# Odd 64 queries of each batch: one 128-query window per pair replaced by paired 64-column tiles

## The chip, the cores and the metric

The kernel runs on one core of one Trainium2 chip. The metric is the device time of one execution in microseconds. Before the change it is 575.62 us, the median of three runs (575.4 to 577.56 us).

## The reference

A query-and-key-normalised attention over 8 batches, 12 heads, 448 tokens and 64 dimensions per head is followed by a low-rank mixer over the tokens and a two-layer MLP with a ReLU.

```python
q_n, k_n = rmsnorm(q, g_q), rmsnorm(k, g_k)
attn = softmax(q_n @ k_n.T / sqrt(64))
x = (attn @ v)                      # (8, 12, 448, 64), then rows of 768 per token
u = x + (x.T @ U @ V).T             # U (448, 32), V (32, 448): mixes tokens
out = u + relu(u @ w_ch1) @ w_ch2   # 768 -> 3072 -> 768
```

## The kernel before

**Tiling.** Heads are taken in pairs (six a batch) and pairs in groups of two. 448 tokens are three blocks of 128 and one of 64. The exponentials of a pair are one tile `E` with the keys on the partitions and the 448 queries in the columns: two slots for each of three key blocks (one per head), and a seventh slot that holds the last 64 keys of both heads on its two halves. Two `E` buffers take turns.

**Attention products.** `products` (L475) multiplies `E` by the values. The stationary operand is a window of 128 query columns of `E`, the moving one the values with a column of ones (65 columns a head, so that the row sums come with it). A window takes seven matmuls: one of 130 columns for the slot with the last keys (L485) and six of 65 columns (L489). Since 448 is not a multiple of 128, there are four windows per pair, and the fourth overlaps its neighbour by 64 queries: `WIN` (L54) starts it at 320 in even batches and at 0 in odd ones. Half of that window's rows are used. One call of `V` (L504) does two windows and then, on DVE, a reciprocal of the sums (L498) and a multiplication into the batch's rows `x` (L499).

**Scores.** From group 6 on (batch 2), `Spair` (L444) does a pair's scores as one stretch of PE: two 64-row matmuls side by side (L450, tiles `sl`), four more in two rounds (L459, tiles `sc`), and one over all 128 rows (L461, a third `sl`). ACT follows with the exponentials: one for each of the first two `sl` (L452), then the last `sl` (L462), then two double tiles (L464). In batch 1 `Srows` does the same in smaller steps (L429, L434), and batch 0 is written out by hand.

**Mixer and MLP.** `mix_t` (L513) multiplies the batch's rows by `U`, in four 32-column tiles side by side (L518); `mix_two` (L525) multiplies by `V` and adds the rows (L541). `up` (L596) makes one block of the hidden layer: six matmuls of 448 columns (L600) into a tile `ph`, then a ReLU on ACT (L607). `down` (L640) makes a tile `po` of 128 tokens by 384 columns from 24 matmuls (L647), given out in four parts of six, and then adds the rows on DVE (L657).

**PSUM.** Two pools: `ps_sc` with two double buffers (for `sc`), and `ps` with four single buffers, which `ph`, `po`, `pv`, `sl` and the mixer's `pu` share. A tile takes a buffer that has been read out, or the one that will be first.

**Order.** All engines are in the order in which the program records instructions. Two lists are merged: `att` (attention steps, each with a cost) and `mlp` (MLP steps of the batch before). A step of `att` is taken when its share is due (`due`) and `ready` (L898) agrees; otherwise the next MLP step is. `ready` looks at running estimates of each engine's time and keeps scores and `V` apart by at least one MLP step. `done_at` holds the place in `att` from which a batch's rows are complete, and no MLP step of the batch is taken before it.

Of the kernel before, what the change touches and what calls it, by code (L numbers as in the profile page):

```python
# [9 lines left out]
FP32 = mybir.dt.float32  # L10
# [10 lines left out]
LEAD = 1.8  # L21
REST = 8.0
SECOND = 53.0


@with_exitstack
def kernel(
# [413 lines left out]
        runs("act", 0.9 if n == 2 else 0.52)  # L441
        exp_done[(b, pr)] = at["act"]

    def Spair(b, pr):  # L444
        qT, kT = qk[divmod(b * NPAIR + pr, 2)]
        E = es[(b, pr)] = ep.tile([P, NB, S], BF16, name="E", tag="E")
        ts = [ps.tile([P, 512], FP32, name="sl", tag="ps")[:, :S] for _ in range(2)]
        for i in range(2):
            d = slice(i * D, (i + 1) * D)
            nc.tensor.matmul(ts[i], kT[d, 2 * P:3 * P], qT[d], start=True, stop=True)  # L450
        for i in range(2):
            nc.scalar.activation(E[:, 4 + i, :], ts[i], AF.Exp, scale=scal, bias=bias)  # L452
        runs("pe", 0.4)
        runs("act", 1.04)
        tiles = [ps_sc.tile([P, 2, 512], FP32, name="sc", tag="sc") for _ in range(2)]
        for r in range(2):
            for i in range(2):
                d = slice(i * D, (i + 1) * D)
                nc.tensor.matmul(tiles[r][:, i, :S], kT[d, r * P:(r + 1) * P], qT[d], start=True, stop=True)  # L459
        last = ps.tile([P, 512], FP32, name="sl", tag="ps")[:, :S]  # L460
        nc.tensor.matmul(last, kT[:, SM:], qT, start=True, stop=True)  # L461
        nc.scalar.activation(E[:, 6, :], last, AF.Exp, scale=scal, bias=bias)  # L462
        for r in range(2):
            nc.scalar.activation(E[:, 2 * r:2 * r + 2, :], tiles[r][:, :, :S], AF.Exp, scale=scal, bias=bias)  # L464
        runs("pe", 0.6)
        runs("act", 2.3)
        exp_done[(b, pr)] = at["act"]

    def Srows(blocks):
        for x in blocks:  # L470
            Sc(*x)

# [31 lines left out]
    def V(b, pr, half):  # L504
# [3 lines left out]
        runs("pe", 0.5)  # L508
        runs("dve", 0.6)

    tTs = {}

    def mix_t(b):  # L513

        pt = ps.tile([P, QC], FP32, name="pu", tag="ps")
        for j in range(NW):
            for g in range(NQ):
                nc.tensor.matmul(pt[g * rank:(g + 1) * rank, :], Ub[:, j if j < NJ else NJ + b % 2, :],  # L518
                                 xs[b][:, j, g * QC:(g + 1) * QC], start=(j == 0), stop=(j == NW - 1))
        tTs[b] = headp.tile([P, QC], BF16, name="tT", tag="tT")  # L520
        nc.vector.tensor_copy(tTs[b], pt)
        runs("pe", 0.6)
        runs("dve", 0.35)

    def mix_two(b, ws):  # L525

        odd = b % 2
        off = 0 if odd else 64
        ts = [ps_sc.tile([P, 2, 512], FP32, name="sc", tag="sc") for _ in range(2)]
        for i, w in enumerate(ws):  # L530
            vc = w * P if w < NJ else (SM if odd else S - P)
            for g in range(NQ):
                r = slice(g * rank, (g + 1) * rank)
                nc.tensor.matmul(ts[g // 2][:, g % 2, i * QC:(i + 1) * QC], Vr[r, vc:vc + P], tTs[b][r], start=True, stop=True)  # L534
        runs("pe", 0.4)
        for i, w in enumerate(ws):
            lo, hi = (0, P) if w < NJ else (0, R) if odd else (R, P)
            full = xs[b][:, w, :] if w < NJ else u_rest[lo:hi, :]
            for half in range(2):
                h = slice(half * HALF, (half + 1) * HALF)  # L540
                nc.vector.tensor_tensor(full[:, h].rearrange("p (g c) -> p g c", g=2),  # L541
                                        ts[half][lo:hi, :, i * QC:(i + 1) * QC],
                                        xs[b][lo:hi, w, h].rearrange("p (g c) -> p g c", g=2), ALU.add)
                runs("dve", 0.56)
            c = off + w * P
            nc.sync.dma_start_transpose(uT[:, :, c:c + hi - lo], full)
# [141 lines left out]
    for i, (b, pr) in enumerate(pairs):  # L688
        if b == 0:
            continue  # L690
        gi, a = divmod(i, 2)
        more = gi + 1 < len(groups)
        by_dma = gi + 1 >= DMA_FROM
        soon = gi + 2 < len(groups)

        if a == 0 and pr == 0 and b > 1:
            add_att(0.5, V, *pairs[i - 1], 0)
            if gi == DMA_FROM:
                add_att(0.0, sums, gi + 1, 0)
                add_att(0.0, sums, gi + 1, 1)  # L700
                add_att(0.0, scale_all, gi + 1)
            add_att(0.5, V, *pairs[i - 1], 1)
        if gi >= DMA_FROM:
            add_att(0.5 if a == 1 and soon else 1.0, Spair, b, pr)
            if a == 0 and more:
                add_att(0.0, turn_dma, gi + 1)
                add_att(0.0, take_dma, gi + 1)
                if gi + 3 < len(groups):
                    add_att(0.0, load, gi + 3)
            if pr != 0:  # L710
                add_att(0.45, V, *pairs[i - 1], 0)
                if a == 1 and soon:
                    add_att(0.0, squares, gi + 2, 0)
                    add_att(0.0, squares, gi + 2, 1)
                add_att(0.45, V, *pairs[i - 1], 1)
                if a == 1 and soon:
                    add_att(0.0, sums, gi + 2, 0)
                    add_att(0.0, sums, gi + 2, 1)
                    add_att(0.5, lambda: None)
                    add_att(0.0, scale_all, gi + 2)  # L720
            continue

        if a == 0:
            add_att(0.45, Srows, ((b, pr, 0), (b, pr, 1)))
            if pr == 0:
                add_att(0.8, lambda: None)
            if not by_dma:
                add_att(0.0, squares, gi + 1, 0, nc.gpsimd)
                add_att(0.0, squares, gi + 1, 1, nc.gpsimd)
                if gi + 2 < DMA_FROM:  # L730
                    add_att(0.0, load, gi + 3)
            if pr != 0:
                add_att(0.4, V, *pairs[i - 1], 0)
                add_att(0.5, V, *pairs[i - 1], 1)
            add_att(0.0, sums, gi + 1, 0)
            add_att(0.0, sums, gi + 1, 1)
            add_att(1.0, Srows, ((b, pr, 2), (b, pr + 1, 0), (b, pr, 3)))
            add_att(0.0, scale_all, gi + 1)
            if gi + 2 == DMA_FROM:
                add_att(0.0, squares, gi + 2, 0, nc.gpsimd)  # L740
                add_att(0.0, squares, gi + 2, 1, nc.gpsimd)
                add_att(0.0, weights, 2)
            add_att(0.4, V, b, pr, 0)
        else:
            add_att(0.6, Srows, ((b, pr, 1), (b, pr, 2), (b, pr, 3)))
            if gi + 2 == DMA_FROM:
                add_att(0.0, load, gi + 3)
            if not by_dma:
                add_att(0.5, V, *pairs[i - 1], 1)
                add_att(0.39, T, gi + 1, 0)  # L750
                add_att(0.39, T, gi + 1, 1)
                continue
            add_att(0.0, squares, gi + 2, 0)
            add_att(0.0, squares, gi + 2, 1)
            add_att(0.5, V, *pairs[i - 1], 1)
            add_att(0.0, turn_dma, gi + 1)
            add_att(0.0, take_dma, gi + 1)
            add_att(0.0, load, gi + 3)
    add_att(0.55, V, *pairs[-1], 0)
    add_att(0.55, V, *pairs[-1], 1)  # L760


    done_at = {0: 0}
    for n, (c, f, a) in enumerate(att):
        if f is V and a[1] == NPAIR - 1 and a[2] == 1:
            done_at[a[0]] = n + 1


    PRE, GAP = (14, 20), (5, 6)
# [89 lines left out]
    for step in FRONT.split():  # L859
        step, _, eng = step.partition(":")  # L860
        name, *a = step.split(".")
        steps[name](*map(int, a), engines[eng])
        if step == "scp.1.0":
            fill_mixer()
        if name == "val":
            load(int(a[0]) + 3)
    weights(2)

    at.update(pe=0.0, act=0.0, dve=0.0)
# [27 lines left out]

    def ready(f, a):  # L898
        if f is Spair:
            if im > 0 and mixes(mlp[im - 1][1]):  # L900
                return False
            return at["dve"] <= at["pe"] + 0.3 and at["act"] <= at["pe"] + 0.6
        if f is V and ca >= a_one and (after_pair or after_v):
            return False
        if f is sums and a[0] > DMA_FROM:
            return not any(m[1] is mix_t for m in mlp[max(0, im - 1):im + 3])
        if ca >= a_one:
            return True
        if f is V:
            return exp_done[a[:2]] <= at["pe"] + 0.1  # L910
        return f is not Srows or at["act"] <= at["pe"] + 0.6

# [1 line left out]
    while ia < len(att) or im < len(mlp):  # L914
# [6 lines left out]
        if take_att:  # L921
# [3 lines left out]
            else:  # L925
                f(*a)
            after_pair = after_pair or f is Spair
            after_v = after_v or f is V
            if ia >= a_from:
                ca += c  # L930
            ia += 1
# [46 lines left out]
```

## Time and profile before

| | us |
|---|---|
| median of three runs | 575.62 |
| the profiled execution | 575.53 |
| its span in the trace | 573.80 |
| PE busy | 564.3 |
| ACT busy | 308.3 |
| POOL busy | 204.9 |
| DVE busy | 196.1 |

The profile gives, for one execution, each engine's busy time, the chain of work that ended last, groups of instructions by line, and a timeline. PE is TensorE's matmuls and PEld its weight loads. A matmul's length in a row (194 ns for 65 columns, 352 ns for 448) is its passage through the array, and matmuls overlap in it; what a matmul costs is the distance from its start to the next one's start. Span and execution differ by 1.73 us that lie around the traced instructions. The granted TensorE clock is 1.0 through the whole span.

### The profile page before, as it was taken

To read this page: it belongs to the slowest core of one execution; us is meant where nothing else is said; L and a number is where in the kernel's file an instruction comes from. 1 tells how busy PE (TensorE), PEld (TensorE's weight loads), DVE (VectorE), ACT (ScalarE), POOL (GpSimd) and SP (SyncE) were. 2 spreads that over 40 slices of the span, in tenths; PEclk is the share of its full clock that TensorE was granted. 3 is DMA by queue.
4 is the path that set the end of the run, shared out by engine and by line. 5 is a ranking of instruction groups with operands and counts; after the bars stand their busy time and mean duration, and the time that the engine had idled before them with its cause. 6 is when DMAs were issued, how large, how long until landed. Compare 5 with 4: busy or idle time off the path is not lost.

```text
span 573.8 us, 11520 instructions
## 1 busy us (share of the span) xinstructions
PE 564.3 (98%) x4720; PEld 325.9 (57%) x4720; DVE 196.1 (34%) x448; ACT 308.3 (54%) x515; POOL 204.9 (36%) x306
## 2 busy tenths in 40 slices
PE   8799999999999999999999999999999999999997
PEld 7565555555655555655556555555565555555565
DVE  7965655312343231621335330443034310410011
ACT  6876770787454876267653578367752444014300
POOL 7873785265323615325524523532531000000000
PEclk9999999999999999999999999999999999999999
DMA  9999999674447743597246835376205210320022
GB/s 234 201 240 239 246 225 225 128 198 83 121 82 163 171 111 45 95 218 165 36 129 106 192 98 131 62 187 145 35 21 99 49 29 1 69 62 1 1 55 57
DMA packets 104829, 68.20 MB, mean 119 GB/s; under 512 B 66632, under 2 KB 100936, under 8 KB 104776
## 3 DMA queue, kind: packets, MB, share of 16 engines
q1 hardware_dynamic: 95124, 57.83, 44.1%
q0 software_dynamic: 9408, 9.44, 9.8%
q8 instruction: 37, 0.61, 0.5%
q10 hardware_dynamic: 244, 0.20, 0.1%
q14 instruction: 16, 0.13, 0.1%
HBM read 52.20 MB, written 11.01 MB: 110 GB/s over the span
## 4 chain that ended last, share of the span: by engine, by line
PE 93%; DMA 3%; ACT 2%; POOL 0%; SPq 0%; issue 0%; DVE 0%; POOLq 0%
PE ph L600 37%; PE po L647 37%; PE pv L489 6%; PE sc L459 2%; PE pv L485 2%; PE sl L461 2%; PE sl L450 2%; ACT E L434 2%; DMA vf<-in_v_dram 2%; DMA qf<-in_q_dram 1%; PE po L634 1%; PE sc L429 1%; PE sc L618 1%; PE sc L534 1%; PE pu L518 1%; PE pt L367 0%
## 5 line engine op out<-in xcount | busy, mean ns | idle before, releaser
L600 PE MATMUL ph<-uT,w1b 128*128 128x448 bf16 x1128 | 225.7, 352 | 0.2 <-ACT E L434 0.2
L647 PE MATMUL po<-w2b,hT 128*128 128x384 bf16 x1296 | 224.2, 326 | 0.0
L647 PEld LDWEIGHTS <-hT 128*128 128x128 bf16 x1296 | 122.7, 98 | 79.0 <-issue 2.8
L600 PEld LDWEIGHTS <-w1b 128*128 128x128 bf16 x1128 | 107.3, 98 | 93.0 <-issue 0.8
L607 ACT ACTIVATE hT<-ph 128x448 bf16<-128x448 f32 x185 | 98.8, 552 | 111.5 <-PE ph L600 109.5
L452 ACT ACTIVATE E<-sl,gg 128x448 bf16<-128x448 f32 x72 | 41.6, 631 | 72.9 <-PE sl L450 72.9
L398 POOL TENSOR_SCALAR qT<-qT,gg 128x448 bf16<-128x448 bf16 x36 | 50.4, 1402 | 82.7 <-DMA qT<-qn 80.0
L498 DVE RECIPROCAL r<-pv 128x4 f32<-128x4 f32 x96 | 17.3, 180 | 175.0 <-PE pv L489 174.9
L197 POOL TENSOR_TENSOR qn<-qf,rs 128x384 bf16<-128x384 f32 x36 | 29.8, 829 | 124.7 <-ACT rs L174 117.8
L464 ACT ACTIVATE E<-sc,gg 128x896 bf16<-128x896 f32 x72 | 69.1, 1025 | 0.0
L657 DVE TENSOR_TENSOR ob<-po,x 128x384 f32<-128x384 f32 x46 | 25.6, 557 | 104.0 <-PE po L647 101.3
L489 PE MATMUL pv<-va,E 128*128 128x65 bf16 x1152 | 57.2, 194 | 0.0
L489 PEld LDWEIGHTS <-E 128*128 128x128 bf16 x1152 | 50.5, 98 | 6.5
L166 DVE TENSOR_REDUCE ssq<-sq 128x14 f32<-128x896 f32 x45 | 46.9, 1078 | 2.4 <-ACT sq L140 2.3
L485 PE MATMUL pv<-vl,E 128*128 128x130 bf16 x192 | 42.2, 220 | 0.3 <-ACT E L434 0.2
L499 DVE TENSOR_TENSOR x<-pv,r 128x256 bf16<-128x256 f32 x96 | 40.7, 424 | 3.3
L434 ACT ACTIVATE E<-sc,gg 128x896 bf16<-128x896 f32 (+1 forms) x42 | 37.1, 952 | 4.8 <-PE sc L429 4.6
L197 POOL TENSOR_TENSOR kp<-kf,rs 128x384 bf16<-128x384 f32 x36 | 29.8, 828 | 0.0
L541 DVE TENSOR_TENSOR x<-sc,x 128x384 bf16<-128x384 f32 x42 | 20.8, 550 | 16.7 <-PE sc L534 16.7
L173 ACT ACTIVATE rs<-ssq,eps 128x28 f32<-128x28 f32 (+1 forms) x24 | 7.5, 313 | 34.0 <-DVE ssq L166 34.0
L485 PEld LDWEIGHTS <-E 128*128 128x128 bf16 x192 | 18.7, 97 | 10.2 <-issue 2.4
L462 ACT ACTIVATE E<-sl,gg 128x448 bf16<-128x448 f32 x36 | 23.0, 639 | 0.0
(110 smaller groups left out, 370.8 us busy)
## 6 DMA issues: line engine op xcount, KB each, us to landing
qf<-in_q_dram SPq DMA_DIRECT2D x23, 448.0 KB, 3.9
kf<-in_k_dram SPq DMA_DIRECT2D x23, 448.0 KB, 5.2
vf<-in_v_dram SPq DMA_DIRECT2D x48, 192.0 KB, 5.5
out_dram<-ob SPq DMA_DIRECT2D x48, 192.0 KB, 2.7
w2b<-in_moe_w_ch_dram POOLq DMA_DIRECT2D x8, 576.0 KB, 13.5
w1b<-in_moe_w_ch_dram POOLq DMA_DIRECT2D x2, 1152.0 KB, 17.0
vf<-in_v_dram SPq DMA_DIRECT2D x48, 32.0 KB, 5.2
w1b<-in_moe_w_ch_dram POOLq DMA_DIRECT2D x1, 1536.0 KB, 28.1
```

Of the source, the lines that this page charges most:

```text
L166: nc.vector.tensor_reduce(ssqs[gi][:, i, :], sqs.pop((gi, i)), AX, ALU.add)
L197: nc.gpsimd.tensor_tensor(main.rearrange("p (t i) d -> p i t d", i=2), src[:, c, :2 * NJ].rearrange("p (i t) d -> p i t d", i=2), rs[:, c, ...
L398: nc.gpsimd.tensor_scalar(qT[:, a], qT[:, a], gg[:, 0:1], None, ALU.mult)
L434: nc.scalar.activation(es[(b, pr)][:, 2 * r:2 * r + n, :], sc[:, :n, :S], AF.Exp, scale=scal, bias=bias)
L452: nc.scalar.activation(E[:, 4 + i, :], ts[i], AF.Exp, scale=scal, bias=bias)
L464: nc.scalar.activation(E[:, 2 * r:2 * r + 2, :], tiles[r][:, :, :S], AF.Exp, scale=scal, bias=bias)
L485: nc.tensor.matmul(pv[:, i].rearrange("p e d -> p (e d)"), E[:, 2 * NJ, w:w + P], vl[:, lp, :], start=True, stop=False)
L489: nc.tensor.matmul(pv[:, i, e, :], E[:, 2 * j + e, w:w + P], va[:, (first_h + step * e) * NJ + j, :], start=False, stop=(e == 1 and j == N ...
L499: nc.vector.tensor_tensor(xs[b].rearrange("p i (h d) -> p i h d", d=D)[:, 2 * half:2 * half + 2, h0:h0 + step + 1:step, :], pv[:, :, :, :D ...
L600: nc.tensor.matmul(ph, w1b[:, dt, ht * P:(ht + 1) * P], uT[:, dt, off:off + S], start=(dt == 0), stop=(dt == KD - 1))
L607: nc.scalar.activation(hT[:, ht, off:off + S], ph, AF.Relu)
L647: nc.tensor.matmul(po, hT[:, ht, col:col + P], w2b[:, ht, half * HALF:(half + 1) * HALF], start=(ht == 0), stop=(ht == KH - 1))
```

## The change

From batch 1 on, a pair's products are three windows of 128 queries instead of four, done in one call (`Vall`) with one reciprocal and one multiplication. The remaining 64 queries are done once per group, for both its pairs, in a new stretch of sixteen matmuls: `rest_products`. There the stationary operand is 64 query columns of `E`, and the two heads of a pair go to the two 64-column halves of the array, so that one tile `pr` holds one head on partitions 0 to 63 and the other on 64 to 127. `rest_norms` puts the results into a tile of their own (`x_rest`, one for even and one for odd batches), from which the mixer and the MLP then read the fourth block. Its other half is cleared once.

The stretch of a group is placed in front of the next group's first score stretch: within `Spair` sixteen times, within `Srows` twice (batch 1), and by itself three times (at the start of batches 2 and 3 and after the last pair). Within `Spair` it is recorded after the first two `sl` tiles are taken and ahead of their matmuls.

```diff
+APART = 3
...
-    def Spair(b, pr):
+    def Spair(b, pr, rest=None):
         qT, kT = qk[divmod(b * NPAIR + pr, 2)]
         E = es[(b, pr)] = ep.tile([P, NB, S], BF16, name="E", tag="E")
         ts = [ps.tile([P, 512], FP32, name="sl", tag="ps")[:, :S] for _ in range(2)]
+        if rest is not None:
+            rest_tile(rest)
+            rest_products(rest)
+            rest_norms(rest)
...
-    def Srows(blocks):
+    def Srows(blocks, rest=None):
+        if rest is not None:
+            Rest(rest)
...
+    x_rest = [consts.tile([P, dm], BF16, name=f"xr{i}") for i in range(2)]
+
+    def products_all(b, pr):
...
+        pv = ps.tile([P, NJ, 2, D1], FP32, name="pv", tag="ps")
+        for i in range(NJ):
+            w = WIN[b % 2][i]
+            nc.tensor.matmul(pv[:, i].rearrange("p e d -> p (e d)"), E[:, 2 * NJ, w:w + P], vl[:, lp, :],
+                             start=True, stop=False)
+            for e in range(2):
+                for j in range(NJ):
+                    nc.tensor.matmul(pv[:, i, e, :], E[:, 2 * j + e, w:w + P],
+                                     va[:, (lp + 2 * e) * NJ + j, :], start=False, stop=(e == 1 and j == NJ - 1))
...
+    def rest_products(gi):
...
+        q0 = 0 if b % 2 else SM
+        for lp in range(2):
+            E = es[divmod(2 * gi + lp, NPAIR)]
+            for j in (NJ, *range(NJ)):
+                for e in range(2):
+                    nc.tensor.matmul(
+                        pv[e * R:(e + 1) * R, lp, :],
+                        E[:, 2 * j + (e if j < NJ else 0), q0:q0 + R],
+                        va[:, (lp + 2 * e) * NJ + j, :] if j < NJ else vl[:, lp, e * D1:(e + 1) * D1],
+                        start=(j == NJ), stop=(j == NJ - 1))
...
+    def rest_norms(gi):
...
+        nc.vector.reciprocal(r, pv[:, :, D])
+        for e in range(2):
...
+            nc.vector.tensor_tensor(
+                x_rest[b % 2][lo:hi, c:c + 2 * D].rearrange("p (h d) -> p h d", d=D),
+                pv[rows, :, :D],
+                r[rows].rearrange("p h -> p h ()").to_broadcast([R, 2, D]), ALU.mult)
...
+    def rest_tile(gi):
+        rest_tiles[gi] = ps.tile([P, 2, D1], FP32, name="pr", tag="ps")
...
+        rest = gi - 1 if a == 0 and (pr > 0 or b > APART) else None
         if a == 0 and pr == 0 and b > 1:
-            add_att(0.5, V, *pairs[i - 1], 0)
+            add_att(0.8, Vall, *pairs[i - 1])
...
-            add_att(0.5, V, *pairs[i - 1], 1)
+            if b <= APART:
+                add_att(0.5, Rest, gi - 1)
         if gi >= DMA_FROM:
-            add_att(0.5 if a == 1 and soon else 1.0, Spair, b, pr)
+            add_att((0.5 if a == 1 and soon else 1.0) + (0.35 if rest is not None else 0.0), Spair, b, pr, rest)
...
+    for i in range(2):
+        nc.gpsimd.memset(x_rest[i][R:] if i else x_rest[i][:R], 0.0)
...
         if f is Spair:
+            if a[2] is not None and mlp[im][1] is down and mlp[im][2][3] > 0:
+                return False
```

More of the change, by code (lines that the diff above doesn't have):

```diff
@@ L509, in V @@
         runs("dve", 0.6)
+    x_rest = [consts.tile([P, dm], BF16, name=f"xr{i}") for i in range(2)]
+    def products_all(b, pr):
+        if b not in xs:
+            xs[b] = xp.tile([P, NW, dm], BF16, name="x", tag="x")
+        gi, lp = divmod(b * NPAIR + pr, 2)
+        va, vl = normed[gi][2:]
+        E = es[(b, pr)]
+        pv = ps.tile([P, NJ, 2, D1], FP32, name="pv", tag="ps")
[7 more added lines that the diff above has]
+                                     va[:, (lp + 2 * e) * NJ + j, :], start=False, stop=(e == 1 and j == NJ - 1))
+        h0 = groups[gi][1] + lp
+        r = headp.tile([P, NJ, 2], FP32, name="r", tag="r")
+        nc.vector.reciprocal(r, pv[:, :, :, D])
+        nc.vector.tensor_tensor(
+            xs[b].rearrange("p i (h d) -> p i h d", d=D)[:, :NJ, h0:h0 + 3:2, :],
+            pv[:, :, :, :D],
+            r.rearrange("p i e -> p i e ()").to_broadcast([P, NJ, 2, D]), ALU.mult)
@@ new lines, in Vall @@
+    def Vall(b, pr):
+        at["pe"] = max(at["pe"], exp_done[(b, pr)])
+        products_all(b, pr)
+        runs("pe", 0.73)
+        runs("dve", 0.75)
+    rest_tiles = {}
+    def rest_products(gi):
+        b = groups[gi][0]
+        va, vl = normed[gi][2:]
+        pv = rest_tiles[gi]
+        q0 = 0 if b % 2 else SM
[8 more added lines that the diff above has]
+                        start=(j == NJ), stop=(j == NJ - 1))
+        runs("pe", 0.36)
@@ new lines, in rest_norms @@
+    def rest_norms(gi):
+        b, h0, _ = groups[gi]
+        pv = rest_tiles.pop(gi)
+        lo, hi = (0, R) if b % 2 else (R, P)
+        r = headp.tile([P, 2], FP32, name="r", tag="r")
+        nc.vector.reciprocal(r, pv[:, :, D])
+        for e in range(2):
+            rows = slice(e * R, (e + 1) * R)
+            c = (h0 + 2 * e) * D
+            nc.vector.tensor_tensor(
+                x_rest[b % 2][lo:hi, c:c + 2 * D].rearrange("p (h d) -> p h d", d=D),
+                pv[rows, :, :D],
+                r[rows].rearrange("p h -> p h ()").to_broadcast([R, 2, D]), ALU.mult)
+        runs("dve", 0.6)
@@ L511, with Rest @@
+    def rest_tile(gi):
+        rest_tiles[gi] = ps.tile([P, 2, D1], FP32, name="pr", tag="ps")
+    def Rest(gi):
+        rest_tile(gi)
+        rest_products(gi)
+        rest_norms(gi)
     tTs = {}
@@ L518, in mix_t @@
                 nc.tensor.matmul(pt[g * rank:(g + 1) * rank, :], Ub[:, j if j < NJ else NJ + b % 2, :],
-                                 xs[b][:, j, g * QC:(g + 1) * QC], start=(j == 0), stop=(j == NW - 1))
+                                 (xs[b][:, j] if j < NJ else x_rest[b % 2])[:, g * QC:(g + 1) * QC],
+                                 start=(j == 0), stop=(j == NW - 1))
         tTs[b] = headp.tile([P, QC], BF16, name="tT", tag="tT")
@@ L542, in mix_two @@
                                         ts[half][lo:hi, :, i * QC:(i + 1) * QC],
-                                        xs[b][lo:hi, w, h].rearrange("p (g c) -> p g c", g=2), ALU.add)
+                                        (xs[b][lo:hi, w, h] if w < NJ else x_rest[odd][lo:hi, h])
+                                        .rearrange("p (g c) -> p g c", g=2), ALU.add)
                 runs("dve", 0.56)
@@ L710 @@
             if pr != 0:
-                add_att(0.45, V, *pairs[i - 1], 0)
+                add_att(0.5, Vall, *pairs[i - 1])
                 if a == 1 and soon:
@@ L714 @@
                     add_att(0.0, squares, gi + 2, 1)
-                add_att(0.45, V, *pairs[i - 1], 1)
+                add_att(0.25, lambda: None)
                 if a == 1 and soon:
@@ L723 @@
         if a == 0:
-            add_att(0.45, Srows, ((b, pr, 0), (b, pr, 1)))
+            add_att(0.45, Srows, ((b, pr, 0), (b, pr, 1)), rest)
             if pr == 0:
@@ L732 @@
             if pr != 0:
-                add_att(0.4, V, *pairs[i - 1], 0)
-                add_att(0.5, V, *pairs[i - 1], 1)
+                add_att(0.9, Vall, *pairs[i - 1])
             add_att(0.0, sums, gi + 1, 0)
@@ L742 @@
                 add_att(0.0, weights, 2)
-            add_att(0.4, V, b, pr, 0)
+            add_att(0.4, lambda: None)
         else:
@@ L748 @@
             if not by_dma:
-                add_att(0.5, V, *pairs[i - 1], 1)
+                add_att(0.5, Vall, *pairs[i - 1])
                 add_att(0.39, T, gi + 1, 0)
@@ L754 @@
             add_att(0.0, squares, gi + 2, 1)
-            add_att(0.5, V, *pairs[i - 1], 1)
+            add_att(0.5, Vall, *pairs[i - 1])
             add_att(0.0, turn_dma, gi + 1)
@@ L758 @@
             add_att(0.0, load, gi + 3)
-    add_att(0.55, V, *pairs[-1], 0)
-    add_att(0.55, V, *pairs[-1], 1)
+    add_att(0.8, Vall, *pairs[-1])
+    add_att(0.3, Rest, len(groups) - 1)
     done_at = {0: 0}
     for n, (c, f, a) in enumerate(att):
-        if f is V and a[1] == NPAIR - 1 and a[2] == 1:
-            done_at[a[0]] = n + 1
+        gi = a[0] if f is Rest else a[2] if f is Spair else None
+        if gi is not None and gi % 3 == 2:
+            done_at[groups[gi][0]] = n + 1
     PRE, GAP = (14, 20), (5, 6)
@@ L902, in ready @@
             return at["dve"] <= at["pe"] + 0.3 and at["act"] <= at["pe"] + 0.6
-        if f is V and ca >= a_one and (after_pair or after_v):
+        if f in (Vall, Rest) and ca >= a_one and (after_pair or after_v):
             return False
@@ L908, in ready @@
             return True
-        if f is V:
+        if f is Vall:
             return exp_done[a[:2]] <= at["pe"] + 0.1
@@ L927 @@
             after_pair = after_pair or f is Spair
-            after_v = after_v or f is V
+            after_v = after_v or f is Vall
             if ia >= a_from:
```

## The prediction

> **What bounds the kernel now.** I read the busy times first, then the chain that ended last, then the busy time by stages.
>
> ```profile
> PE 564.3 (98%) x4720; PEld 325.9 (57%) x4720; DVE 196.1 (34%) x448; ACT 308.3 (54%) x515; POOL 204.9 (36%) x306
> ...
> PE 93%; DMA 3%; ACT 2%; POOL 0%; SPq 0%; issue 0%; DVE 0%; POOLq 0%
> ...
> 85.00:468.90 383.90, 383.90 (x3242) 217.57 (x3241) 126.26 (x277) 224.97 (x377) 146.26 (x230) 1.00 0.53 117
> ```
>
> The last row is a stretch of 383.90 us in which PE (the second number) is busy for all of it. Nearly all of the change lies there, so its cost is what it adds to PE's sequence: distances between matmul starts, plus waits that PE does not have today. The timeline prices each kind of stretch.
>
> ```profile
> 334.47 0.22 PE L485 MATMUL pv<-vl,E 128*128 128x130 bf16 x1
> 334.52 0.35 PE L489 MATMUL pv<-va,E 128*128 128x65 bf16 x6
> 334.71 0.22 PE L485 MATMUL pv<-vl,E 128*128 128x130 bf16 x1
> 334.77 0.35 PE L489 MATMUL pv<-va,E 128*128 128x65 bf16 x6
> 334.95 0.35 PE L600 MATMUL ph<-uT,w1b 128*128 128x448 bf16 x1
> ...
> 90.63 0.81 PE L647 MATMUL po<-w2b,hT 128*128 128x384 bf16 x4
> 91.37 0.51 PE L518 MATMUL pu<-x,Ub 128*32 128x192 bf16 x16
> 91.82 0.50 PE L647 MATMUL po<-w2b,hT 128*128 128x384 bf16 x2
> ...
> 101.47 0.36 PE L450 MATMUL sl<-qT,kT 64*128 64x448 bf16 x2
> ...
> 101.66 0.54 PE L459 MATMUL sc<-qT,kT 64*128 64x448 bf16 x4
> 101.86 1.16 ACT L452 ACTIVATE E<-sl,gg 128x448 bf16<-128x448 f32 x2 [11.54 <-PE sl L450]
> ...
> 102.14 0.36 PE L461 MATMUL sl<-qT,kT 128*128 128x448 bf16 x1
> ...
> 102.34 0.49 PE L647 MATMUL po<-w2b,hT 128*128 128x384 bf16 x2
> ...
> 6.87 0.38 PE L284 MATMUL pg<-ob 1*128 1x1 f32 x2
> 7.11 0.36 PE L285 MATMUL pg<-ob 1*128 1x1 f32 x2
> ```
>
> First block: two windows take 334.47 to 334.95, and over all windows the starts give 246 ns each (57 ns for the 130 columns, 31.7 ns for each 65). Second: the form `128*32` marks column tiles. Third: a score stretch, with 0.40 us from its first matmul to the first exponential. Fourth: single-column matmuls with nothing between them but weight loads.
>
> **What it removes.** The fourth window of each pair in batches 1 to 7: 42 windows x 0.246 = **-10.35 us**. The other three cost the same in one call as in two, since stretches of this shape follow each other and the MLP without a gap.
>
> **What it adds: the tiled stretch.** 21 groups, each sixteen matmuls of 65 columns in eight rounds of two heads. In L518 the four tiles of a round start 3 to 4 ns apart and the next round 83 ns later, about the time of 192 columns: column tiles do run side by side. So streaming alone allows a round the 32 ns of one L489 matmul. The weight loads are the open size. A full 128-column load hides under those 32 ns, and its row shows it read in four strips of 32. A 64-column load has no such row. Bounds: 32 ns below (loads stay hidden); above, 83 ns, since a round of L518 loads the same 128 columns in all within that. The nearest row for a load read as one strip is L284 and L285: their matmuls stream one column, and start 133, 112 and 111 ns apart, which is the load of 128 columns; it also lasts 182 ns in its row against 98 ns for the strip kind. Half as many columns at that pace are 56 ns. Two such loads one after the other would be 111 ns, more than the 83 ns just given, so I take them as parallel: **56 ns a round**, 21 x 8 x 0.056 = **+9.41 us**.
>
> The Trainium skill speaks against this change here: "TensorEngine Tiling (Array Packing)", section Restrictions, says that column tiling switches the fast weight load off, and "TensorE: Matmul & The Clock Gate", section on LDWEIGHTS, puts a plain load at columns over 1.2, some 53 ns for 64. The sum by that would be 0.5 us lower than mine; the L284 rows agree with it within 3 ns.
>
> **What it adds: mode changes.** From the last po at full width to L518 the starts are 256 ns apart where 163 is the po's own, and back 178 ns where 83 is the round's, plus 10 ns on the next: about 96 ns in, 105 out. The same shows around the 64-row scores (258 and 285 ns in, 282 out). Where the new stretch stands ahead of scores, their own entry was paid before, so one change is added: 18 x 0.096 = 1.73 us (from column to row tiles no trace shows a change; between 0 and the full 0.096, and I take the full one, as every other pair of modes has it). Three stretches stand alone: 3 x 0.201 = 0.60 us. Together **+2.3 us**.
>
> **What it adds: waits for a PSUM buffer.** I followed in the changed program which instruction each PE wait names. `ps` has four buffers. Before, a score stretch took three, and what came next found one that had been free for long. Now it takes four (two `sl`, `pr`, the last `sl`), so the tile after the first `sl` by four must wait until its exponential (L457 there) has read it out. There are two kinds among the sixteen:
> - Ten times the stretch is followed by a new `ph` or `po`, and its first matmul names that exponential. Today it starts 0.87 us after the first score matmul (101.47 to 102.34). The exponential starts at 0.40 and lasts 0.63 (its group's mean), so it ends at 1.03; in the five places where a matmul waited for ACT, it began 51 ns after ACT's end. So 1.08 instead of 0.87: 0.21 us.
> - Six times a `po` is half done and holds a buffer; the rule added to `ready` looks only at the next MLP step, which there is a mixer step. Then the last `sl` itself names the exponential, and would start at 1.08 instead of 0.67 (101.47 to 102.14): 0.41 us.
>
> 10 x 0.21 + 6 x 0.41 = **+4.54 us**. Everything behind it on PE moves by as much, and in this stage PE has no slack. The ReLU of the `ph` ahead (0.55 us, which today delays some of these exponentials by 0.15) is over by then, as the tiled stretch lies between. Every other wait that the change gives PE is for something over a microsecond of PE work back.
>
> **Costed at nothing.** DVE: a reciprocal and multiplication less per pair, against three small ones per group; it is 34% busy, and has 1 us between `pr` and the first `mix_t` that reads it; without that cover, its 0.18 + 2 x 0.21 us (half of L499's 0.42) once a batch. POOL: two memsets at about 33 us, some 0.8 us each by the 0.52 us of the 128x512 one at 8.96 us, ahead of two weight transfers first needed at 80 us; behind them its next product sat idle 2.0 us. Without that cover 1.6 us, once. SP's transfers move with their steps and gain none. In batch 1 `pr` stands between the transposes and the scores that wait for the copied keys; by the same wait today (0.46 us, once) it is 0.2 us, twice. The merging of the lists shifts steps there; I allow 0.5 us either way.
>
> **Sum.** -10.35 + 9.41 + 1.73 + 0.60 + 4.54 = +5.9 us. On the profiled execution's 575.53 (span 573.80 and 1.73 around it; 0.1 below the median) this is **581.5 us**.
>
> **Rivals.**
> - *Loads stay hidden.* A round is 32 ns: 168 x 0.024 = 4.0 us less, 577.4. For it: 128 columns hide today, and L518's 32-column loads do not show. Against: those are strips or a quarter as wide. [...]
> - *The halves do not run side by side*, so the change doesn't do what it says: two 31.7 ns a round, 63 ns, +7.1 us, 582.6; or loads queue up to 83 ns a round, +10.5, 586.0. Against: L518.
> - *Not slower, by the PSUM buffers.* If PE did not wait for the exponentials in fact, because a tile is let go before the exponential's recorded end, 4.54 us come back: 576.9 with 56 ns a round, 572.9 with 32, and 571.2 if the change from column to row tiles is free as well. At 32 ns a round it turns to faster where the sixteen waits mean less than 2.64 / 16 = 0.165 us each. For it: the two kinds of wait are read from the program, not from a trace. Against: a matmul began 51 ns after the recorded end in all five places seen.
>
> **How the numbers follow.** The measurement can tell about 0.5% (2.9 us) from no change. Forecast with 56 to 63 ns a round, 0.62, within 579.5 to 583.5. Loads hidden, 0.20, at 577.4, and waits absent at 576.9 or 572.9, 0.04: all within 0.5%. Loads queueing, 0.08, about 586. Waits absent, loads hidden and a free change, 0.06, at 571.2. So slower 0.70, same 0.24, faster 0.06. The range takes in the forecast's and the hidden loads' and leaves out the ends: 576.0 to 584.0, about 0.84.
>
> **What would show it.** Starts of the new matmuls (L560) some 56 ns apart by rounds, sixteen in about 0.45 us, and 0.096 us more than a round ahead of the first score. PE waiting for ACT L457 ten times at `ph` or `po` with 0.2 us and six times at the third `sl` (L466) with 0.4. If rounds take 32 ns or PE shows no such waits, the sum is wrong by the amounts above; if PE's busy share falls outside score stretches, a wait that I did not find is there.

## The result and the profile after

The changed kernel takes 578.46 us (median of 21 runs, 576.37 to 580.69), the kernel before 575.40 us beside it (21 runs, 574.41 to 579.09). The ratio is **1.0046, with a 95% interval from 1.0030 to 1.0062**: 2.65 us slower by the ratio, where 5.9 us had been forecast. The profiled execution took 579.34 us, with a span of 577.60 (before 575.53 and 573.80). Of the runs further down, two executions of e1_apart fell into a slower state and are left out of its time: 652.13 us, the profiled one, and 1158.65 us.

These are the rows of the page's busy times, of its chain that ended last, and of the same stretch of 383.90 us as before (the second number is PE's busy time).

```profile
PE 564.9 (98%) x4762; PEld 323.2 (56%) x4762; DVE 191.2 (33%) x426; ACT 308.3 (53%) x516; POOL 206.2 (36%) x308
...
PE 80%; DMA 9%; ACT 3%; POOL 3%; issue 3%; SPq 0%; DVE 0%; POOLq 0%; ACTq 0%
...
85.00:468.90 383.90, 379.60 (x3208) 211.38 (x3205) 123.12 (x255) 221.76 (x372) 144.88 (x226) 1.00 0.53 118
```

PE's busy time has hardly moved (564.3 to 564.9), but in the stretch where it had no hole it now stands idle for 4.3 us. The chain leaves PE more often too: 9% of it is DMA, where it was 3%, since it is now followed back through a load of second-layer weights to the transfers at the front. The waits of PE name the holes (columns: us in total, times, longest).

```profile
PE sl L466 <- ACT E L457: 2.1, 6, 0.4
PE busy L245 <- POOL ident masks.py:199: 1.4, 1, 1.4
PE sc L430 <- ACT E L435: 1.1, 5, 0.3
...
PE po L728 <- DMA w2b<-in_moe_w_ch_dram: 1.0, 1, 1.0
PE ph L681 <- DMA uT<-u_rest: 0.7, 1, 0.7
```

The first row is one of the two kinds of wait that the prediction named. The other kind is too short a hole for this view: in the trace itself PE is idle ten times for 45 to 47 ns ahead of a `ph` or `po`, and each of these holes names the same exponential (L457). The last two rows the prediction did not name. Now the timeline around one new stretch that is followed by a new `ph` (start, us, engine, line):

```profile
115.91 0.22 PE L560 MATMUL pr<-vl,E 128*64 128x65 bf16 x2
115.97 0.26 PE L560 MATMUL pr<-va,E 128*64 128x65 bf16 x6
116.06 0.20 PE L560 MATMUL pr<-vl,E 128*64 128x65 bf16 x2
116.10 0.26 PE L560 MATMUL pr<-va,E 128*64 128x65 bf16 x6
116.29 0.36 PE L455 MATMUL sl<-qT,kT 64*128 64x448 bf16 x2
116.49 0.54 PE L464 MATMUL sc<-qT,kT 64*128 64x448 bf16 x4
116.69 1.16 ACT L457 ACTIVATE E<-sl,gg 128x448 bf16<-128x448 f32 x2
116.97 0.36 PE L466 MATMUL sl<-qT,kT 128*128 128x448 bf16 x1
117.38 0.92 PE L681 MATMUL ph<-uT,w1b 128*128 128x448 bf16 x4
```

Sixteen matmuls take from 115.91 to 116.29, with the step to the scores: 0.38 us, where the prediction needs 0.45 for the sixteen alone. In the trace the first rounds start 52 ns apart and the later ones 29 to 36, the two heads of a round 0 to 7 ns apart. The new `ph` starts 1.09 us after the first score matmul and 0.41 after the third `sl` (116.97 to 117.38); where no tile is missing that last distance is 0.20. Here is one of the other six, where a half-done `po` holds a buffer:

```profile
173.10 0.36 PE L455 MATMUL sl<-qT,kT 64*128 64x448 bf16 x2
173.30 0.54 PE L464 MATMUL sc<-qT,kT 64*128 64x448 bf16 x4
...
173.50 1.16 ACT L457 ACTIVATE E<-sl,gg 128x448 bf16<-128x448 f32 x2 [0.38 <-PE sl L455]
174.18 0.35 PE L466 MATMUL sl<-qT,kT 128*128 128x448 bf16 x1 [0.34 <-ACT E L457]
174.37 1.14 PE L728 MATMUL po<-w2b,hT 128*128 128x384 bf16 x6
```

The third `sl` starts 1.08 us after the first, with the wait written behind it. All sixteen of these matmuls start 51 or 52 ns after the end of the exponential that the prediction named. And this is where the other two waits lie:

```profile
97.45 0.81 PE L728 MATMUL po<-w2b,hT 128*128 128x384 bf16 x4 [1.03 <-DMA w2b<-in_moe_w_ch_dram]
...
107.62 1.21 SPq L627 DMA_TRANSPOSE uT<-u_rest  x1
...
110.15 0.54 PE L681 MATMUL ph<-uT,w1b 128*128 128x448 bf16 x2 [0.71 <-DMA uT<-u_rest]
```

A `po` wants the last part of the second-layer weights, whose last packet ends at 97.03 us (93.36 in the trace of before). Later PE wants the transposed tile of the rest rows, whose transfer SP issued at 107.62. By the distances between matmul starts the two cost 1.19 and 0.87 us, 2.06 together.

### The profile page after: what moved, and what is told of

It is laid out like the page before. It is cut to its first block, busy times and chain, and to the rows that moved or that the text cites. A ratio compares the mean times of both kernels' runs of the same rounds, so it can differ in the third digit from the quotient of the medians.

```text
span 577.6 us, 11577 instructions
## 1 busy us (share of the span) xinstructions
PE 564.9 (98%) x4762; PEld 323.2 (56%) x4762; DVE 191.2 (33%) x426; ACT 308.3 (53%) x516; POOL 206.2 (36%) x308
## 4 chain that ended last, share of the span: by engine, by line
PE 80%; DMA 9%; ACT 3%; POOL 3%; issue 3%; SPq 0%; DVE 0%; POOLq 0%; ACTq 0%
PE po L728 34%; PE ph L681 33%; DMA kf<-in_k_dram 6%; PE pv L533 3%; DMA w2b<-in_moe_w_ch_dram 3%; PE sl L455 2%; ACT E L457 2%; POOL sq L144 2%; ACT E L435 1%; PE sl L466 1%; PE po L715 1%; PE sc L464 1%; PE pr L560 1%; PE pv L529 1%; PE sc L614 1%
## 5 line engine op out<-in xcount | busy, mean ns | idle before, releaser
L681 PE MATMUL ph<-uT,w1b 128*128 128x448 bf16 x1128 | 223.1, 352 | 1.1 <-DMA uT<-u_rest 0.7
L728 PE MATMUL po<-w2b,hT 128*128 128x384 bf16 x1296 | 221.9, 326 | 1.1 <-DMA w2b<-in_moe_w_ch_dram 1.0
L681 PEld LDWEIGHTS <-w1b 128*128 128x128 bf16 x1128 | 108.5, 98 | 98.7 <-issue 3.8
L457 ACT ACTIVATE E<-sl,gg 128x448 bf16<-128x448 f32 x72 | 41.6, 630 | 79.2 <-PE sl L455 78.1
L537 DVE RECIPROCAL r<-pv 128x6 f32<-128x6 f32 x42 | 8.2, 195 | 124.2 <-PE pv L533 123.9
L533 PE MATMUL pv<-va,E 128*128 128x65 bf16 x756 | 35.4, 194 | 0.0
L533 PEld LDWEIGHTS <-E 128*128 128x128 bf16 x756 | 32.4, 98 | 3.4
L529 PE MATMUL pv<-vl,E 128*128 128x130 bf16 x126 | 27.6, 219 | 0.0
L538 DVE TENSOR_TENSOR x<-pv,r 128x384 bf16<-128x384 f32 x42 | 23.4, 557 | 1.4
L206 POOL CAST va<-vf 128x768 bf16<-128x768 f32 x24 | 20.7, 861 | 1.2 <-DMA vf<-in_v_dram 1.2
```

Of the source, the lines that this page charges most:

```text
L529: nc.tensor.matmul(pv[:, i].rearrange("p e d -> p (e d)"), E[:, 2 * NJ, w:w + P], vl[:, lp, :], start=True, stop=False)
L533: nc.tensor.matmul(pv[:, i, e, :], E[:, 2 * j + e, w:w + P], va[:, (lp + 2 * e) * NJ + j, :], start=False, stop=(e == 1 and j == NJ - 1))
L681: nc.tensor.matmul(ph, w1b[:, dt, ht * P:(ht + 1) * P], uT[:, dt, off:off + S], start=(dt == 0), stop=(dt == KD - 1))
L728: nc.tensor.matmul(po, hT[:, ht, col:col + P], w2b[:, ht, half * HALF:(half + 1) * HALF], start=(ht == 0), stop=(ht == KH - 1))
```

## The experiments

Two theories on the sum: the sixteen waits cost what was booked and the rounds are shorter than booked (called A in most of what follows), or the waits are hidden in part and something else made the time. The runs are ordered by the question that they answer.

**Are the waits and the mode changes worth what was booked?** In e1_apart every tiled stretch stands alone, in the place the change already uses for some of them, so no score stretch asks for a fourth buffer.

```diff
-        rest = gi - 1 if a == 0 and (pr > 0 or b > APART) else None
+        rest = None
+        late = gi - 1 if a == 0 and (pr > 0 or b > 1) and i > NPAIR else None
...
-            if b <= APART:
-                add_att(0.5, Rest, gi - 1)
+        if late is not None:
+            add_att(0.5, Rest, late)
```

> The changed kernel with every tiled stretch by itself, at least one MLP step away from the scores. Theory A (the sum of the prediction holds but for the weight loads: PSUM waits 4.54 us, one mode change 0.1 us): the sixteen waits for the exponential go, 4.5 us, and sixteen stretches pay a second mode change, 16 x 0.105 = 1.7 us, so 2.8 us less than the changed kernel, about 575.6. PE waits for ACT L457 are gone from the trace. Theory B (the waits only take up time that PE would lose anyway; the rest of the loss is the late w2b transfer and what follows it, 2.1 us in the changed kernel's trace): 1.7 us more than the changed kernel, about 580.2.

Measured: 575.94 us (10 runs), ratio to before 1.0007 [0.9989, 1.0026]. That is the time of A. Its trace, taken at a granted clock of 0.85, has no wait of PE for L457; e3_between below shows the same at a clock of 1.00. With the waits goes the changed kernel's loss against before.

**Can the same be had with the stretch still beside the scores?** e3_between puts it between the side-by-side scores and the last `sl`, so that the exponentials of the first two `sl` run under it. There the new pair's exponentials are recorded ahead of the stretch's reads of the old ones, and it needs a third buffer for E. c3_three_e is therefore the control: the changed kernel with that third buffer, and with the rest's rows kept in `x`, cleared batch by batch, in place of the two memsets ahead of the weights.

```diff
-    ep = ctx.enter_context(tc.tile_pool(name="ep", bufs=2))
+    ep = ctx.enter_context(tc.tile_pool(name="ep", bufs=3))
...
-    x_rest = [consts.tile([P, dm], BF16, name=f"xr{i}") for i in range(2)]
+    def x_rest(b):
+        return xs[b][:, NJ]
...
-    for i in range(2):
-        nc.gpsimd.memset(x_rest[i][R:] if i else x_rest[i][:R], 0.0)
```

> A control for e3_between: the changed kernel with a third E buffer, and with the tiled stretch's rows put into the fourth window of x (its other half cleared by GpSimd, once a batch, 0.8 us) instead of a tile of their own. No order on PE changes, so both theories expect the changed kernel's time, 578.5 within 0.7, and all sixteen waits for ACT L457.

Measured: 578.49 us (12 runs), 1.0035 [1.0011, 1.0059], like the changed kernel, with all sixteen waits. Neither the E buffers nor the memsets carry the loss. On top of it, e3_between moves the tiled stretch from ahead of the scores to behind the loop over `sc`:

```diff
-        if rest is not None:
-            rest_tile(rest)
-            rest_products(rest)
-            rest_norms(rest)
...
+        if rest is not None:
+            rest_tile(rest)
+            rest_products(rest)
+            rest_norms(rest)
```

> As c3_three_e, but the tiled stretch stands between the side-by-side scores and the last full-width one, and takes its PSUM buffer there. The number of mode changes is the same. The next tile then begins at about 1.25 us after the first score matmul, past the 1.08 at which the first exponential has let its buffer go, and the last score at 1.05 to 1.08. Theory A: the sixteen waits go without a second mode change: 4.54 less 6 x 0.03, 4.4 us less than c3_three_e, about 574.0, faster than before by 1.4. Theory B (the waits cost nothing by themselves): no change against c3_three_e.

Measured: **574.44 us** (12 runs), 0.9973 [0.9954, 0.9993] of before. It is 4.05 us under its control, where 4.4 were expected, and faster than both kernels. Its timeline at the same place, and its row of the stretch from 85 us on:

```profile
115.52 0.36 PE L451 MATMUL sl<-qT,kT 64*128 64x448 bf16 x2
115.72 0.54 PE L460 MATMUL sc<-qT,kT 64*128 64x448 bf16 x4
116.07 1.15 ACT L453 ACTIVATE E<-sl,gg 128x448 bf16<-128x448 f32 x2
116.19 0.22 PE L562 MATMUL pr<-vl,E 128*64 128x65 bf16 x2
...
116.57 0.36 PE L466 MATMUL sl<-qT,kT 128*128 128x448 bf16 x1
116.77 3.57 PE L682 MATMUL ph<-uT,w1b 128*128 128x448 bf16 x18
```

```profile
85.00:468.90 383.90, 382.53 (x3263) 213.88 (x3260) 124.03 (x257) 223.03 (x376) 149.45 (x232) 1.00 0.54 117
```

From the third `sl` to the new `ph` it is 0.20 us again, and of the idle 4.3 us in the stretch 1.4 are left, about what this execution waited for the two transfers (0.6 and 0.8 in its waits).

**How long is a round, and why?** In e2_turns the recorded order is one head after the other, to take the side-by-side run of the halves away.

```diff
-            for j in (NJ, *range(NJ)):
-                for e in range(2):
+            for e in range(2):
+                for j in (NJ, *range(NJ)):
```

> The changed kernel with the two halves of the array in turns: eight matmuls of one head, then eight of the other, twice. If it is the running side by side that makes the stretch cheap (theory A, eight rounds of 33 ns): sixteen starts 31 ns apart, 0.50 instead of 0.28 us a stretch, 21 x 0.22 = 4.6 us more than the changed kernel, about 583. If the loads are the limit and streams overlap in any order (theory B): unchanged, about 578.5.

Measured: 578.23 us (12 runs), 1.0037 [1.0014, 1.0059]: unchanged, so the expectation of A failed. But the trace shows why it doesn't speak against side-by-side halves: the first matmul of the second half starts 14 ns after that of the first, although three others stand between them in the recorded order (both are `pr<-vl`, the product that is recorded first for each head). PE ran both halves together in spite of the order, in 280 ns a stretch instead of 253. The edit did not take away what it was meant to, so the sizes were measured by themselves: the probe adds runs of 24 small matmuls behind the kernel's end, with the identity as weights, and leaves the rest as it was.

> The kernel before with stretches of 24 matmuls added after its last one, their output unused: 64-column tiles in two halves with 8 and with 65 moving columns, the same in one half only, 32-column tiles in four quarters with 8, then 96, 120 and 128 stationary columns with 8, and 128 with 65. With 8 moving columns only the weight load can set the distance. Theory A (the pace read from L284, 128 columns in 111 ns, was that of f32; bf16 in one strip loads twice as fast, one column in 0.42 ns): 64 columns 27 to 30 ns a round, 96 columns 42, 120 columns 52, 128 columns in four strips about 25. Theory B (the pace of the prediction, 0.87 ns a column, and the tiled stretch escapes it by loading ahead): 64 columns 56 ns, 96 columns 83, 120 columns 104. One half only with 65 moving columns: 31 ns a matmul by A, so twice the time of two halves.

Measured: 588.0 us, of which only the added matmuls matter. Part of their timeline, the matmuls at full width between them left out (the form is rows*columns of the tile; the second shape is what streams):

```profile
573.78 0.55 PE L957 MATMUL probe<-ident 128*64 128x8 bf16 x24
...
574.69 0.57 PE L960 MATMUL probe<-ident 128*64 128x65 bf16 x24
...
575.63 0.92 PE L963 MATMUL probe<-ident 128*64 128x8 bf16 x24
...
576.93 0.94 PE L966 MATMUL probe<-ident 128*64 128x65 bf16 x24
...
578.84 1.20 PE L972 MATMUL probe<-ident 128*96 128x8 bf16 x24
...
580.23 1.43 PE L975 MATMUL probe<-ident 128*120 128x8 bf16 x24
```

L957 and L960 take turns between two halves, L963 and L966 stay in one. With eight columns streaming, a matmul in one half starts every 31.7 ns behind the first: that is its weight load of 64 columns. Wider loads read as one strip give 45 ns at 96 columns and 55 at 120, so 24 columns take 10 ns: 0.417 ns a column and some 5 ns on top. With the kernel's 65 columns streaming, one half gives 31.9 ns. Two halves by turns give 32 ns for a round of two, whether 8 or 65 columns stream. So the halves' loads run beside each other, and a load of 64 columns takes just as long as 65 columns stream. The "loads stay hidden" rival had the round right.

**Is the rest of the difference the late weights?** fill_before and fill_after put 54 idle matmuls, about 3.0 us, ahead of the first step that uses the second-layer weights, in the kernel before and in the changed one.

```diff
+                if b == c == part == 0:
+                    mlp.append((0.0, keep_busy, (54,), 0))
```

> The kernel before with 54 more unused matmuls of 128 columns (3.0 us of PE) ahead of the first down step, so that the second layer's weights have 3 us longer to arrive. With no late weights in most runs of before: 575.4 + 3.0 = 578.4. If before itself waits for them in a part of its runs, up to 0.5 less.

> The changed kernel with the same 3.0 us of PE work ahead of the first down step. If part of the measured difference is late weights (2.1 us in the changed kernel's profiled execution, none in before's), it falls from 2.7 to about 1.7 against fill_before: 580.1. If the whole difference is PE's own sequence and its waits for ACT, it stays at 2.7: 581.1.

Measured: 578.39 us (12 runs) and 579.90 (6 runs), that is 1.0044 [1.0024, 1.0064] and 1.0069 [1.0043, 1.0096] of the kernel before. The medians differ by 1.5 us, which is nearer to the 1.7 of late weights, but the intervals overlap too much to settle it. The traces say it better: neither has a wait for `w2b` or `u_rest`, and from PE's first `ph` matmul to its last matmul they take 531.65 and 533.33 us, 1.67 apart. The changed kernel itself was then profiled three times more.

> The changed kernel as it is, profiled once more. Theory A (late second-layer weights are the part of the cost that differs from execution to execution): the profiled execution's time less the waits of PE for w2b and for the copied tile of the rest (u_rest), with what they push back, is the same in every profile: 579.34 - 2.07 = 577.3 in the first. So an execution with both waits takes 578.5 to 580, one without them 576.5 to 577.5. Theory B (the spread has another cause): time and these two waits do not go together.

> As the run before it: a second look at the changed kernel. A: time less the two waits and what they push back is 577.3 within 0.5. B: it differs by over 1.

> As the two runs before it: a third look at the changed kernel. A: time less the two waits and what they push back is 577.3 within 0.5. B: it differs by over 1.

Measured: 576.24, 576.83 and 577.03 us. The same distance, from the first `ph` to the last matmul, goes with the waits, to 0.01 us in the four profiles of the changed kernel:

| profiled execution | time, us | last packet of the second-layer weights ends at | waits for `w2b` and `u_rest`, by matmul starts | first `ph` to last matmul | less the waits |
|---|---|---|---|---|---|
| before | 575.53 | 93.36 | none | 528.63 | 528.63 |
| changed, first | 579.34 | 97.03 | 1.19 + 0.87 | 532.37 | 530.30 |
| again1 | 576.24 | 93.30 | none | 530.30 | 530.30 |
| again2 | 576.83 | 93.79 | none | 530.31 | 530.31 |
| again3 | 577.03 | 94.21 | 0 + 0.71 | 531.02 | 530.31 |
| c3_three_e | 578.45 | 96.09 | 0.45 + 0.94 | 531.85 | 530.46 |
| e3_between | 574.73 | 96.54 | 0.76 + 0.94 | 527.82 | 526.13 |

By the whole time the expectation of A (577.3 within 0.5 after the waits are taken off) failed in two of the three executions: 576.2, 576.8 and 576.3. The reason is that the front of the kernel, ahead of the first `ph`, also varies: it took 40.3 us in again1 and 41.5 in the first profile. The last column is what the change costs in each of its profiles: **1.67 us**. The rest of the 2.65 is not split. Late transfers (0 to 2.1 us here) are in it. So may be the granted clock: six of the changed kernel's 21 executions had 0.997, with a median of 579.77 us against 577.46 for the others, and 7 of 35 executions of the kernel before had 0.997 or less, with 578.17 against 575.25. No run separates the two.

again3 has the second wait without the first. Its tile of the rest rows was written as early as in again1, 59.08 us behind the first `ph`, but SP issued the transfer at 64.74 instead of 63.84. So the second wait is not only the first one handed on; what held SP back stays open.

**Could the planner avoid the longer kind of wait?** The change's rule in `ready` looks only at the very next MLP step. e5_rule lets it look past a mixer step.

```diff
-            if a[2] is not None and mlp[im][1] is down and mlp[im][2][3] > 0:
+            nxt = next((m for m in mlp[im:] if m[1] in (up, down)), None)
+            if a[2] is not None and nxt is not None and nxt[1] is down and nxt[2][3] > 0:
```

> The changed kernel with the rule in ready looking past a mixer step to the next up or down step, so that no score stretch with a tiled one starts while a po is half done. All sixteen waits are then of the kind ahead of a new ph, 0.21 us; the six of 0.41 at the third sl go. Theory A: 6 x 0.2 = 1.2 us less than the changed kernel, 577.3. Theory B (waits of either kind cost nothing by themselves): unchanged.

Measured: 581.35 us (6 runs), 1.0106 [1.0073, 1.0138]: 2.9 us slower than the changed kernel instead of about 1 faster, so the expectation of A failed and B's too. From the first `ph` to the last matmul its trace takes 534.82 us, 4.5 more than the changed kernel without late transfers. Of its waits of PE, these two are new:

```profile
PE ph L681 <- ACT hT L688: 2.2, 2, 1.1
PE ph L681 <- DVE x L538: 2.0, 2, 1.0
```

The six waits of the third `sl` are gone, as they should be. As I read the timeline, the steps held back now crowd into the places where `ph` is built, and at other times nothing of attention is left to lie between two `ph`; no run tests this reading. The timeline shows PE with only first-layer work, which ReLU cannot follow:

```profile
330.00 1.39 ACT L688 ACTIVATE hT<-ph 128x448 bf16<-128x448 f32 x3
...
330.58 0.73 PE L681 MATMUL ph<-uT,w1b 128*128 128x448 bf16 x3 [1.11 <-ACT hT L688]
```

The two new waits add up to 4.2 us. Moving work in time to avoid the six waits cost more than it gave.

## Why the prediction was off, step by step

- **Bound by PE's sequence:** right. What the change costs is found in distances between matmul starts and in new waits of PE, and nowhere else.
- **The removed windows, -10.35 us:** right. By their starts the attention windows (`pv`) take 41.53 us behind the first `ph` before and 30.96 in again1, -10.57 us.
- **The tiled stretch, 56 ns a round, +9.41 us: this step failed.** The new rounds start at 0, 52, 88, 121, 153, 184, 215 and 250 ns: the first takes 52 and the others 33 on average, so with the last stream a stretch takes 0.285 us and the 21 take 5.96. The term was 3.45 us too large. The row chosen was the wrong one: L284 and L285 load f32 weights, and 128 columns of them take 111 ns, 0.87 ns a column. The bf16 load read as one strip takes 0.417 ns a column. It isn't the clock: the 128-column matmuls just ahead of L284 and behind L285 start 56 ns apart, as later ones of this shape do. (Those before 4.3 us start 107 ns apart, so the full clock that the profile gives for the whole span does not hold for them.) The two loads differ in data type and in rows (1 against 128); whether the factor of two lies in the f32 load, in the f32 matmul behind it or in the single row was not separated. The nearest row by shape of the read (one strip) was taken, and it was the wrong one by a factor of two. The prediction took the agreement of those rows with a page as support: the Trainium skill's "TensorE: Matmul & The Clock Gate", section on LDWEIGHTS, puts 64 columns at some 53 ns, and the probe measured 32. The same page's section on packing small matmuls puts some 4 ns between concurrent tiles; the two heads of the first rounds start 3 to 4 ns apart.
- **That the halves run side by side:** right; the probe gives 32 ns for a round of two, and 32 ns for each single matmul in one half alone.
- **Mode changes, +2.33 us:** right. Measured by the starts, 2.26. The stretch enters at 256 and 282 ns behind a `po` or `ph`, and from column to row tiles it pays too: 126 to 128 ns to the first `sl`, some 95 more than a round.
- **PSUM waits, 10 x 0.21 + 6 x 0.41 = +4.54 us:** right, in number, place and size. In the trace the third `sl` starts 0.41 us late six times (690 ns after the last side-by-side scores instead of 282; one time 750), and the next `ph` or `po` 0.21 late ten times (408 instead of 200). e3_between shows that they are the lever: without them the time falls by 4.05 us.
- **Batch 1, within 0.5 us:** about right. Three short waits of before (0.46, 0.19 and 0.26 us) are gone and 0.29 is new, -0.6.
- **Transfers costed at nothing:** wrong in part. The cover for the second-layer weights was given by their first use, at 80 us. Their last part is used later, at 97.09 us in the profile of before, 3.7 us behind its last packet, and nothing in the prediction looked at that margin. The change itself shortens it: without a wait the changed kernel uses the part 54.7 us behind the first `ph`, 0.9 us sooner than before, and the last packet ends between 93.3 and 97.0 us. c3_three_e has none of the two memsets in front of these weights and shows the wait as well, so the memsets named in the prediction are not needed for it. What makes the last packets land 3 us later in some executions stays open.

The sum of the measured terms is -10.57 + 5.96 + 2.26 + 4.6 - 0.6 = +1.65 us, against 1.67 measured in the trace. The late transfers add between 0 and 2.1 us. The sign and the range held; the size came out at less than half of what was forecast, mainly because of the one row (3.45 us). That the measured 2.65 lies nearer to the forecast than 1.67 is luck: what the prediction had at nothing made up for part of the term that it had too large.

## What to carry to other kernels

Before pricing an operation that the trace lacks by a neighbour, list in what the neighbour differs (shape, data type, order of reading) and keep both neighbours as cases of like weight if each differs in one. When a step takes one more PSUM buffer than the pool has free, count which instruction must let it go and when: here that count gave the waits to some 10 ns, and placing the step later in the same block removed them, where shifting steps by a planner's rule made it worse. For a transfer, the cover ends at the use of its last part, not of its first.

## What the runs showed of the hardware that was not expected

- A bf16 weight load read as one strip takes 0.417 ns a column plus about 5 ns (32, 45 and 55 ns for 64, 96 and 120 columns). 128 columns read in four strips gave 25 ns a matmul in the same probe as long as the granted clock was 1.00 (from 582.0 us on it was 0.50). The Trainium skill's "TensorEngine Tiling (Array Packing)", section Restrictions, has column tiling give up the fast weight load. The two paces agree with that, but for a 64-column load under 65 streaming columns the loss is hidden.
- With 64-column tiles the first round behind a change of tile mode takes 52 or 53 ns, the next ones 32 to 33 on average, in all 21 stretches and in the probe.
- Matmuls on different column tiles need not start in the recorded order: in e2_turns the fifth of a stretch started second, 14 ns after the first.
